# Which bank or buffer a tile gets: one tag for a whole ring, or one tag for each buffer

## The chip, the cores and the metric

The kernel runs on 1 core of one Trainium2 chip. The metric is device time in microseconds (us) of that core: 1204.38 us, the median of 3 runs (1204.35 to 1204.39). One more execution was profiled. It took 1205.93 us, and the span of its trace, from the first instruction to the last, is 1204.2 us.

## The reference

Two stages follow each other. The first is attention with pooled queries, for 8 batches and 8 heads, 1152 keys and head dimension 64:

```python
q_pool = q.reshape(B, H, S // 2, 2, D).mean(axis=3)          # 576 queries
scores = scale * np.matmul(q_pool, k.transpose(0, 1, 3, 2))
attn = exp(scores - max) / (sum + 1e-09)
attn_out = np.matmul(attn, v)                                # 8 x 8 x 576 x 64
```

The second takes the heads side by side as x (8 x 576 x 512). Each of 4 experts projects x to q, k and v of width 64, does causal attention and projects back to 512. A gate picks 2 of the 4 experts for each row and weighs them:

```python
logits = x @ w_gate; topk = the 2 largest; w = softmax over those 2
for e in range(4):
    ye = causal_softmax(scale * (x @ wq[e]) @ (x @ wk[e]).T) @ (x @ wv[e]) @ wo[e]
    out += (e in topk) * w_e * ye
```

## The kernel before, in words

**Tiling.** Heads go in 32 pairs (4 per batch). For each pair the kernel finds row maxima of rough scores (TensorE writes 128x384 tiles, VectorE reduces them, L572), then computes the scores transposed in 9 chunks of 128 keys (L325, as products of split operands qh, ql, kh, kl), exponentiates them on ScalarE into SBUF tiles called pt (L666), multiplies pt by v on TensorE (L332) and adds the pt tiles up on GpSimd into sacc (L349), for the denominators. The queries of a pair are done in two parts of 256 and 320 (QB). The end of a part takes three steps: ScalarE copies the accumulated product out of its PSUM bank into accs (L336); a second bank, den, receives the denominators, their inverse and then the product with accs (VectorE, L345); ScalarE casts den to the high half of x (L336), and VectorE subtracts that from den to get the low half of x (L345). That subtraction is the last reader of the den bank.

**The second stage.** When a batch's four pairs are there, `f_qk` projects x to the experts' queries and keys (L316, 12 matmuls for a tile, four of x's pairs times three terms; the tiles are cast to mqh and mkh). For two experts at a time it makes query and key tiles of 256 columns, then of 320. `f_mmax` (L930) computes score tiles for the row maxima, each in a bank of its own, which VectorE reduces (L956, L960). Causal attention and the output projection follow with the same helpers as in the first stage. Work on one batch's second stage is mixed with the first stage of the next pairs.

**Buffers.** Every kind of tile has a `Ring` (L128): a tag, a shape and a number of buffers. The ring `gen` has 8 buffers of 128x512 float32, which are the 8 PSUM banks: every matmul result lives in one of them. Other rings lie in SBUF: pt (11 buffers), sacc (3), kh (8), v (6) and so on.

**The order of the work.** The kernel is written out by hand. Python generators (`Flow`) stand for the steps. A loop at the end of the kernel function keeps a clock for each engine (`clk`), adds an estimated cost for every instruction it emits (`emit`, L255), and always takes the flow that can go next by these clocks. The framework runs under `tc.manual_schedule()`, so each engine gets its instructions in the order of emission. `emit` notes in each tile's record when the tile was last used by its clocks and by which engine (`u`, `ue`); `ru` is that time plus a delay for the semaphore (0.15 to 0.2 us by the table SEM). For three kinds of VectorE instruction (`port=True`, among them the subtractions that make ql and the sum of qraw, each with two operands in SBUF) `emit` moves the start behind the GpSimd instruction that its clocks show running.

When a step is through with a tile it calls `free()`, which puts the buffer's last times on the ring's list `slots`. A new tile takes the smallest entry of that list, and the clocks go on as if it had got that buffer:

```python
t = min(self.slots)
r = Res(self.pool.tile(self.shape, self.dt, tag=self.tag, name=f"{self.tag}_{self.n}", bufs=self.bufs), self)
_, r.u, r.ue = t
```

The entry holds times only. Which of the ring's buffers the tile really gets is decided by the framework, which knows the tag and the number of buffers, and keeps a timing of its own. The instruction that first writes the tile waits, by semaphore, until the former tile of the buffer that it really got has been used for the last time.

Of the kernel before, what the change touches and what calls it, by code (L numbers as in the profile page):

```python
# [104 lines left out]
class Res:  # L105


    def __init__(self, ap, ring=None):
        self.ap, self.ring, self.w, self.u = ap, ring, 0.0, 0.0
        self.we = self.ue = ""  # L110
# [10 lines left out]
        return self.u + SEM[self.ue]  # L121

    def free(self):
        self.ring.slots.append((self.ru, self.u, self.ue))
        self.ring.live -= 1


class Ring:  # L128
    def __init__(self, pool, tag, shape, dt, bufs):
        self.pool, self.tag, self.shape, self.dt, self.bufs = pool, tag, shape, dt, bufs  # L130
        self.slots, self.live, self.n = [(0.0, 0.0, "")] * bufs, 0, 0

    def avail(self, k=1):
        return sorted(self.slots)[k - 1][0] if len(self.slots) >= k else INF
# [1 line left out]
    def new(self):  # L136
        t = min(self.slots)
        self.slots.remove(t)
        self.live += 1
        self.n += 1  # L140
        r = Res(self.pool.tile(self.shape, self.dt, tag=self.tag, name=f"{self.tag}_{self.n}", bufs=self.bufs), self)
        _, r.u, r.ue = t
        return r


# [1055 lines left out]
```

## Time and profile before

| | |
|---|---|
| median of 3 runs | 1204.38 us (1204.35 to 1204.39) |
| the profiled execution | 1205.93 us, its span 1204.2 us |
| TensorE matmul (PE) busy | 1158.4 us, 96% |
| VectorE (DVE) busy | 860.6 us, 71% |
| ScalarE (ACT) busy | 704.5 us, 58% |
| GpSimd (POOL) busy | 972.0 us, 81% |
| granted TensorE clock | 0.996 of full speed |

PEld is TensorE's loading of weights, which overlaps its matmuls. The ends of matmuls are modelled, so TensorE's 96% does not mean that it could not do more in the time. A stretch in which one engine waits is worth something only if the chain of waits that ends last goes through it.

### The profile page before, as it was taken

Reading aid. Unit: us, or ns where it says so; the run is one execution under the profiler, and the core shown is the slowest. Engines: PE = TensorE matmul, PEld = TensorE weight load, DVE = VectorE, ACT = ScalarE, POOL = GpSimd, SP = SyncE. Lnnn points to the kernel's source line nnn. Section 1 sums busy time; section 2 is a strip of 40 time slices with the busy share of each in tenths; the row PEclk is TensorE's granted clock in tenths of the full one; section 3 lists DMA queues with packets and bytes.
Section 4 is the critical chain, followed back from the end, with each engine's and each line's share of the span. In section 5 each row is a group of like instructions: output and inputs, shape, how many; then the busy total and the mean of one; then the engine's idle time right before and its main releaser. Section 6 shows DMA issues by size and latency. Waiting matters only on the chain.

```text
span 1204.2 us, 29456 instructions
## 1 busy us (share of the span) xinstructions
PE 1158.4 (96%) x11233; PEld 892.0 (74%) x11233; DVE 860.6 (71%) x2113; ACT 704.5 (58%) x2036; POOL 972.0 (81%) x844
## 2 busy tenths in 40 slices
PE   6999999999999999999999999999999999999997
PEld 5676886778876787767886777866877677877785
DVE  7988667767676767777677776776767876577265
ACT  5676545765466654665556754566646665465624
POOL 4999978797699966999669987699786996889912
PEclk9999998999999999999999999999999999999999
DMA  4232212022211212122111221112211122200001
GB/s 158 80 102 69 61 54 67 16 66 76 61 54 55 69 48 61 54 60 92 32 41 54 85 82 30 44 47 85 78 41 34 60 65 87 61 15 9 8 29 45
DMA packets 40426, 70.30 MB, mean 58 GB/s; under 512 B 4871, under 2 KB 31453, under 8 KB 40285
## 3 DMA queue, kind: packets, MB, share of 16 engines
q1 hardware_dynamic: 40284, 68.43, 18.5%
q8 instruction: 88, 1.44, 0.5%
q14 instruction: 54, 0.43, 0.1%
HBM read 58.73 MB, written 9.44 MB: 57 GB/s over the span
## 4 chain that ended last, share of the span: by engine, by line
PE 61%; POOL 27%; DVE 5%; ACT 3%; issue 3%; DMA 1%; POOLq 0%; SPq 0%; DVEq 0%; ACTq 0%
PE gen L325 24%; POOL sacc L349 23%; PE gen L316 19%; PE gen L332 17%; POOL kl L349 3%; ACT pt L666 2%; POOL pt L1018 1%; DVE gen L956 1%; DVE PM L572 1%; DVE ql L345 1%; ACT pt L999 1%; PE gen L622 0%; DVE gen L734 0%; DMA qraw<-in_qT 0%; DVE gen L345 0%
## 5 line engine op out<-in xcount | busy, mean ns | idle before, releaser
L349 POOL TENSOR_TENSOR sacc<-sacc,pt 128x640 f32<-128x640 f32 (+4 forms) x588 | 828.2, 1413 | 128.6 <-ACT sacc L341 92.4
L572 DVE TENSOR_REDUCE PM<-gen 128x1 f32<-128x384 f32 x864 | 425.6, 549 | 168.7 <-PE gen L325 140.3
L666 ACT ACTIVATE pt<-gen 128x320 f32<-128x320 f32 (+1 forms) x1152 | 381.4, 432 | 137.1 <-PE gen L325 126.9
L332 PE MATMUL gen<-pt,v 128*64 128x320 f32 (+4 forms) x2752 | 355.7, 402 | 1.7 <-POOL pt L1018 0.5
L332 PEld LDWEIGHTS gen<-pt,v 128*64 128x64 f32 (+1 forms) x2752 | 192.1, 137 | 138.9 <-issue 11.8
L325 PE MATMUL gen<-qh,kh 64*128 64x320 f32 (+1 forms) x1152 | 211.8, 316 | 2.7 <-ACT accs L336 1.1
L325 PE MATMUL gen<-qh,kl 64*128 64x320 f32 (+1 forms) x1152 | 196.3, 297 | 0.0
L325 PE MATMUL gen<-RM,ON 64*128 64x320 f32 (+1 forms) x1152 | 191.6, 292 | 0.8 <-ACT RM L336 0.8
L325 PE MATMUL gen<-ql,kh 64*128 64x320 f32 (+1 forms) x1152 | 191.3, 293 | 0.0
L325 PE MATMUL gen<-kh,qh 64*128 64x384 f32 x768 | 157.1, 368 | 7.4 <-ACT qh L336 7.1
L325 PEld LDWEIGHTS gen<-qh,kh 64*128 64x128 f32 x1152 | 132.8, 185 | 33.8 <-issue 11.3
L325 PEld LDWEIGHTS gen<-RM,ON 64*128 64x128 f32 x1152 | 130.4, 186 | 1.2 <-ACT RM L336 1.0
L325 PEld LDWEIGHTS gen<-ql,kh 64*128 64x128 f32 x1152 | 129.8, 186 | 0.0
L325 PEld LDWEIGHTS gen<-qh,kl 64*128 64x128 f32 x1152 | 127.4, 186 | 0.0
L325 PEld LDWEIGHTS gen<-kh,qh 64*128 64x128 f32 x768 | 88.2, 187 | 38.1 <-issue 16.3
L316 PE MATMUL gen<-x,WH 128*128 128x320 f32 (+1 forms) x512 | 104.9, 299 | 7.4 <-DVE x L345 7.4
L349 POOL TENSOR_TENSOR kl<-kraw,kh 128x384 fp32r<-128x384 f32 x96 | 95.5, 1013 | 9.5 <-ACT mqh L336 3.4
L956 DVE CUSTOM_DVE_ANT_0 gen<-gen,mqk 64x288 f32<-64x288 f32 (+4 forms) x160 | 74.7, 503 | 25.6 <-PE gen L325 24.4
L316 PEld LDWEIGHTS gen<-x,WH 128*128 128x128 f32 x512 | 82.2, 188 | 10.6 <-issue 9.7
L332 PE MATMUL gen<-sacc,ones 128*64 128x320 f32 (+1 forms) x384 | 66.1, 425 | 13.8 <-POOL sacc L349 13.3
L336 ACT CAST x<-gen 128x256 fp32r<-128x256 f32 x64 | 25.8, 403 | 86.9 <-DVE gen L345 86.8
L316 PE MATMUL gen<-x,WL 128*128 128x320 f32 (+1 forms) x256 | 75.6, 295 | 0.0
(116 smaller groups left out, 1573.5 us busy)
## 6 DMA issues: line engine op xcount, KB each, us to landing
kraw<-in_kT SPq DMA_DIRECT2D x96, 192.0 KB
v<-in_vP SPq DMA_DIRECT2D x96, 192.0 KB
qraw<-in_qT SPq DMA_DIRECT2D x31, 576.0 KB
out<-ob SPq DMA_DIRECT2D x28, 256.0 KB
wst<-in_wall SPq DMA_DIRECT2D x8, 193.0 KB
out<-pt SPq DMA_DIRECT2D x4, 256.0 KB
RM<-nt SPq DMA_DIRECT2D x62, 2.5 KB
out<-ob SPq DMA_DIRECT2D x6, 128.0 KB
```

The costliest lines, as they stand in the source:

```text
L316: nc.tensor.matmul(o, lhsT, rhs, start=start, stop=stop)
L325: nc.tensor.matmul(o(j), l(HEAD[j]), r(HEAD[j]), start=i == 0, stop=i == len(terms) - 1)
L332: nc.tensor.matmul(o(HEAD[j]), l(j), r(j), start=start, stop=stop)
L336: nc.scalar.copy(o, i)
L345: nc.vector.tensor_tensor(o, a, b, op=op)
L349: nc.gpsimd.tensor_tensor(o, a, b, op=op)
L572: nc.vector.tensor_reduce(pm[:, i, t:t + 1], ps[:, :384], axis=AX.X, op=ALU.max)
L666: nc.scalar.activation(pts[i][:, j, :qn], st[j][:, qn * i:qn * i + qn], AF.Exp, scale=0.0625)
L956: nc.vector.tensor_tensor_reduce(p, p, mqk[:m, 384 + m - w:384 + m], 1.0, LOW, ALU.add, ALU.max, pm[:m, j, c, i:i + 1])
L999: nc.scalar.activation(pt_[:kn, j, f:qn], st[j][:kn, o - n:o], AF.Exp, scale=0.125)
L1018: nc.gpsimd.affine_select(out=sq, in_=sq, compare_op=ALU.is_ge, fill=0.0, base=0, pattern=[[0, 2], [1, kn]], channel_multiplier=-1)
```

## The change

A ring's list of free buffers now holds the buffer's number beside its times. A new tile is asked for under the tag of its ring plus that number, with one buffer under that tag. So the framework has nothing to choose: the tile gets the buffer whose entry was smallest by the emission's clocks. This holds for every ring. The smallest entry is the same as before, since the number only stands last in it, and so no clock changes, nor does the order in which instructions are emitted.

```diff
     def free(self):
-        self.ring.slots.append((self.ru, self.u, self.ue))
+        self.ring.slots.append((self.ru, self.u, self.ue, self.slot))
         self.ring.live -= 1
...
-        self.slots, self.live, self.n = [(0.0, 0.0, "")] * bufs, 0, 0
+        self.slots, self.live, self.n = [(0.0, 0.0, "", i) for i in range(bufs)], 0, 0
...
-        r = Res(self.pool.tile(self.shape, self.dt, tag=self.tag, name=f"{self.tag}_{self.n}", bufs=self.bufs), self)
-        _, r.u, r.ue = t
+
+        r = Res(self.pool.tile(self.shape, self.dt, tag=f"{self.tag}{t[3]}", name=f"{self.tag}_{self.n}", bufs=1), self)
+        _, r.u, r.ue, r.slot = t
         return r
```

## Rows read from the trace of the kernel before

**Rows 1.** The page: span, busy time by engine, chain that ended last by engine

```profile
span 1204.2 us, 29456 instructions
...
PE 1158.4 (96%) x11233; PEld 892.0 (74%) x11233; DVE 860.6 (71%) x2113; ACT 704.5 (58%) x2036; POOL 972.0 (81%) x844
...
PE 61%; POOL 27%; DVE 5%; ACT 3%; issue 3%; DMA 1%; POOLq 0%; SPq 0%; DVEq 0%; ACTq 0%
```

**Rows 2.** The waits: engine, line, released by: us in total, times, longest

```profile
PEld gen L325 <- issue: 33.0, 93, 0.5
...
PEld gen L325 <- DVE PM L572: 11.8, 49, 0.5
...
ACT pt L666 <- POOL sacc L349: 7.9, 9, 1.4
...
PE gen L316 <- DVE x L345: 7.4, 6, 1.2
PEld gen L325 <- ACT accs L336: 7.3, 15, 0.5
...
PEld gen L316 <- ACT pt L666: 5.5, 20, 0.5
...
PEld gen L622 <- ACT pt L666: 5.1, 20, 0.4
```

**Rows 3.** TensorE's timeline, 720 to 757 us: start us, us, instructions [idle before]

```profile
741.49 0.41 PE L316 MATMUL gen<-x,WH 128*128 128x256 f32 x2
...
749.36 0.76 PE L325 MATMUL gen<-mkh,mqh 64*128 64x512 f32 x6
751.36 0.47 PE L316 MATMUL gen<-x,WH 128*128 128x256 f32 x2 [1.24 <-DVE x L345]
...
752.87 0.45 PE L316 MATMUL gen<-x,WH 128*128 128x320 f32 x2
...
754.64 0.47 PE L316 MATMUL gen<-x,WH 128*128 128x320 f32 x2
...
756.41 0.27 PE L622 MATMUL gen<-ident,nm 128*10 128x128 f32 x1
```

**Rows 4.** VectorE's timeline, 747 to 757 us

```profile
748.72 0.43 DVE L345 TENSOR_TENSOR gen<-accs,gen 128x256 f32<-128x256 f32 x1
749.06 1.82 DVE L345 TENSOR_TENSOR ql<-qraw,qh 128x576 fp32r<-128x576 f32 x1
750.80 0.41 DVE L345 TENSOR_TENSOR x<-gen,x 128x256 fp32r<-128x256 f32 x1
751.14 0.68 DVE L956 CUSTOM_DVE_ANT_0 gen<-gen,mqk 128x512 f32<-128x512 f32 x1
...
754.08 0.17 DVE L618 TENSOR_REDUCE nm<-MPM 128x10 f32<-128x20 f32 x1
```

**Rows 5.** ScalarE's timeline, 747 to 757 us

```profile
749.24 0.37 ACT L336 CAST x<-gen 128x256 fp32r<-128x256 f32 x1 [1.95 <-DVE gen L345]
749.51 0.43 ACT L336 COPY accs<-gen 128x320 f32<-128x320 f32 x1
```

**Rows 6.** GpSimd's timeline, 749.2 us, and 744 to 900 us

```profile
748.71 1.55 POOL L349 TENSOR_TENSOR sacc<-sacc,pt 128x640 f32<-128x640 f32 x1
...
762.58 0.23 POOL L871 TENSOR_TENSOR gate<-v,gate 128x20 f32<-128x20 f32 x1 [5.36 <-DVE gate L871]
...
768.32 1.27 POOL L349 TENSOR_TENSOR sacc<-sacc,pt 128x512 f32<-128x512 f32 x1 [1.20 <-ACT sacc L341]
```

**Rows 7.** The chain that ended last, 744 to 770 us, and at the start

```profile
8.02 6.64 DVE PM L572 x15
...
749.15 1.73 DVE ql L345
750.88 0.34 DVE x L345
...
751.36 5.21 PE gen L316 x36
```

**Rows 8.** Groups of instructions, shapes apart: busy us, mean ns, idle before

```profile
L345 DVE TENSOR_TENSOR ql<-qraw,qh 128x576 fp32r<-128x576 f32 x31 | 39.7, 1279 | 5.6 <-PE gen L325 2.6 <-ACT qh L336 2.5
```

## The prediction, on record before the changed kernel ran

> **What bounds the kernel now.** I read the page first, then the waits, then the timeline of each engine around one wait, then the chain. The page shows matmuls busy for 1158.4 of 1204.2 us, GpSimd as the next engine with 972.0, and a chain that is 61% TensorE and 27% GpSimd [rows 1]. So time is to be had only where TensorE stands still, or where a stretch of GpSimd on the chain starts late. TensorE is idle for 1204.2 - 1158.4 = 45.8 us in all, lead-in and end included.
>
> The change concerns waits of one kind only: a tile's first writer waits until the former tile in its bank or buffer has been read. In the waits these are the rows in which TensorE waits for a reader of `gen` [rows 2]. For the weight loads they sum to 11.8 + 7.3 + 5.5 + 5.1 = 29.7 us in 49 + 15 + 20 + 20 = 104 waits, 0.29 us each. For the matmuls one row stands out: 7.4 us in 6 waits for "DVE x L345", 1.2 us each. Six waits of one length are one place that comes back in each batch's round.
>
> That place needs the timelines. The reader is to see this at 751.36: six matmuls of a row-max step begin at 749.36, and TensorE then idles 1.24 us, from 750.12 to 751.36, until VectorE has made the low half of x (750.80, 0.41 us) [rows 3, 4]. By its names this is a wait for data, but the data had been there. The matmul at 751.36 projects 256 columns of x, and a projection of the same columns ran at 741.49 [rows 3]: by `f_qk` the tiles of an expert pair come as queries 256, keys 256, queries 320, keys 320, and all of a batch's x must be there for the 320 columns. The x made at 750.80 is for the next batch. What that instruction also does is to read the den bank for the last time. So the projection got den's bank, and waited for it.
>
> Was another bank free? There are 8. Six hold the row-max tiles, which VectorE starts to read only at 751.14, behind the subtraction [rows 4]. The seventh is den. The eighth held a product that ScalarE copied into accs from 749.51 to 749.94 [rows 5], before TensorE had even ended its six matmuls. So a free bank stood unused for 751.36 - 749.94 = 1.42 us.
>
> **The change part by part.** *Instructions.* None is added, removed or moved. The number stands last in the list's entry, so the smallest entry has the same times, and the emission's clocks and its order stay as they are. SP's and GpSimd's queues keep their order too. What can change is which semaphore a first writer waits for, and when it is reached.
>
> *The six places: -7.4 us.* Which bank do the clocks take at 751.36? Both free ones are on the list, so it is the one with the earlier `ru`. I follow the emission's rules from the end of den's product (748.72 + 0.43 = 749.15 [rows 4]). ScalarE's cast of x and the copy into accs follow back to back, so accs is done within 0.8 us (749.94 [rows 5]). VectorE first makes ql, marked `port=True`. Measured, it took 1.82 us against a mean of 1.279 us [rows 4, 8], and it ended 0.62 us after the GpSimd addition of 748.71, whose 1.55 us ran to 750.26 [rows 6]. `emit` copies this: it puts such an instruction behind the GpSimd instruction that it holds to be running. Then comes the subtraction. So den's entry should be about 1.2 us later than that of the copied bank, and the clocks take the copied bank. The projection can then start when TensorE gets to it, at 750.12. Gain: the whole gap, 1.24 us, six times, 7.4 us.
>
> *Is something else late next?* The next tile, 12 matmuls on (752.87 - 751.36 = 1.51 us), would start at 751.63 and take den's bank, read by 751.21. The third would start at 754.64 - 1.24 = 753.40 and takes a row-max bank that VectorE starts to read at 751.14 and holds 0.68 us. The transposition at 756.41 would come at 755.17, and its operand nm is there at 754.08 + 0.17 = 754.25 [rows 3, 4]. So nothing takes the wait's place in the next 5 us. Is it on the path that sets the end? The chain runs through ql, the subtraction and then 36 projections of 5.21 us [rows 7]. GpSimd, the other engine on the chain, is idle behind this place: 5.36 us ended by the gate at 762.58 and 1.20 us ended by ScalarE's first sacc at 768.32 [rows 6], both fed by TensorE. It starts its next long stretch earlier with TensorE. I count the gain in full.
>
> *All other bank picks: 0, between -29.7 and +29.7 us.* The 104 waits of weight loads [rows 2] could go altogether, or as many could come. Both rules hand out the buffer that was free first, one by the framework's timing and one by the emission's. They differ only where two engines free banks within some tenths of a us. Weight loads run ahead of matmuls, so much of these waits is not TensorE's time. I take 0, near to what the rule gives in a steady state, and for the range 15 waits of 0.29 us either way, 4.3 us.
>
> *SBUF rings: 0, between -7.9 and +7.9 us.* The row that bears on them is ScalarE waiting for a pt buffer that GpSimd reads: 7.9 us in 9 waits [rows 2]. ScalarE is busy 58% [rows 1], and GpSimd's own work is what the den matmuls wait for at such times. If this cover were gone the row would be the price. Rings that one engine frees in order (kh, kl, sacc) should get the same buffers as before.
>
> *Second waits: 0, between -33.0 and +33.0 us.* A writer whose bank was read by two engines may need a further semaphore instruction. The nearest row is weight loads idle for no traced reason, 33.0 us in 93 places, 0.35 us each [rows 2]. I see no reason for a shift in the number: the same tiles with the same readers follow each other.
>
> The sum is -7.4 us against the span of 1204.2 us. The profiled execution took 1205.93 us, 1.5 us more than the median of the runs, and the median lies 0.2 us above the span. So I take the gain from the median: 1204.4 - 7.4 = 1197.0 us.
>
> **The rivals.** *The clocks choose the same bank at the six places: 1204.4 us.* For it: without the hold behind GpSimd the emission's costs would put ql at 0.67 and the subtraction at 0.34 us, so den would be done at 749.15 + 1.01 = 750.16, only 0.2 us behind the copy. A shift of the clocks of that size would turn the order where the hold is short. Against it: GpSimd works without a pause there, so the hold is there, and it is 1.1 us in the trace.
>
> The Trainium skill, Perfetto Trace Analysis, Optimization Strategy, speaks against the change too: a gap that comes back the same on the engine that should be busy can mean that there isn't PSUM enough for the next tile. By that rule the gap would stay, whichever bank is chosen, and the time too, 1204.4 us. The trace does not agree for these six: one bank was read by 749.94. For the other bank waits it may hold.
>
> *The gain is given back at GpSimd: about 1203.5 us.* GpSimd has 27% of the chain. If its long stretches began no earlier, TensorE would only wait longer for sacc. Against it stand the 5.36 and 1.20 us of idle time that end with TensorE's work.
>
> *More banks are picked better: 1192.7 us.* The 7.4 us and 15 of the 104 waits: 1204.4 - 7.4 - 4.3.
>
> *Slower: the clocks trust VectorE too early.* Place: the row-max tiles of each pair, where VectorE frees one bank per reduction, 6.64 us / 15 = 0.44 us apart [rows 7]. ql costs 0.67 us on the clocks and 1.279 us on the chip [rows 8]. Where the hold does not cover the difference, VectorE's banks look free 0.6 us before they are, the clocks prefer them to ScalarE's, and TensorE gets its bank one reduction late. Once for each of 32 pairs that is 32 x 0.44 = 14.1 us, less 7.4: 1211.1 us. It decides from 17 such waits on (7.4 / 0.44). Against it: reductions and copies on the clocks have costs near the measured ones, and VectorE's stalls come from GpSimd, which the hold is there for.
>
> **How the numbers follow.** Forecast as worked out, 1195 to 1200 us: 0.55. More banks picked better: 0.10. Same bank at the six places or all banks in use: 0.16. Given back: 0.04. Slower: 0.15. A measurement of this kernel can tell about 0.2%, 2.4 us, from no change. Faster by more: 0.55 + 0.10 = 0.65. Within: 0.16 + 0.04 = 0.20. Slower: 0.15. The range goes from 1192.7 up to the case of no change with half a us on it, 1192.7 to 1205.0; it leaves out the slower case and a little more at the low end. The likeliest case's own range is 1195 to 1200.
>
> **What would show it.** Right: the row of TensorE waiting for "DVE x L345" is gone or below 1 us, the chain has no ql ahead of the projections any more, matmuls are as busy as before in a span 7 us shorter, and GpSimd's idle time ahead of the gate is no longer than before. Wrong in the first step: the row still stands with 6 waits. Wrong in the second: the row is gone, but weight loads' waits for row-max readers grow above 11.8 us by as much, or TensorE's waits for sacc do. A time above 1205 with the row gone would mean new waits elsewhere.

## The result, and the profile after

The changed kernel takes 1193.16 us (median of 4 runs, 1191.78 to 1195.37), the kernel before on the same chip 1204.39 us (4 runs, 1204.35 to 1204.52). The ratio is 0.9909, with a 95% interval of 0.9893 to 0.9924: 11.2 us faster, where 7.4 were forecast. The time lies within the range, below the likeliest case's own range of 1195 to 1200.

Both kernels issue the same instructions in the same order on every engine. There are 21 semaphore instructions fewer (29456 to 29435). What differs is which buffer a tile gets: counted in the two programs, 787 of the 2472 `gen` tiles and 97 of the 693 `pt` tiles follow another tile in their buffer than before, and no tile of any other ring.

The page of the changed kernel, to be held against [rows 1]:

```profile
span 1191.3 us, 29435 instructions
...
PE 1153.4 (97%) x11233; PEld 891.0 (75%) x11233; DVE 855.8 (72%) x2113; ACT 704.0 (59%) x2036; POOL 974.6 (82%) x844
...
PE 64%; POOL 25%; ACT 4%; DVE 3%; issue 3%; DMA 0%; POOLq 0%; SPq 0%; ACTq 0%; DVEq 0%
```

The span is 12.9 us shorter. TensorE is idle for 1191.3 - 1153.4 = 37.9 us, 7.9 less than before, and its matmuls count as busy 5.0 us less. That second number matters below: not all of the gain was in a gap that one could see.

The waits of the changed kernel (engine, line, released by: us in total, times, longest; its lines are one further down than in [rows 2]):

```profile
PEld gen L326 <- issue: 31.5, 89, 0.5
...
PE gen L333 <- POOL sacc L350: 13.4, 16, 1.6
...
PEld gen L326 <- DVE PM L573: 7.6, 32, 0.5
...
PEld gen L326 <- ACT pt L667: 4.5, 12, 1.7
...
PEld gen L623 <- ACT pt L667: 3.1, 14, 0.2
ACT pt L667 <- POOL sacc L350: 3.0, 4, 1.4
PEld gen L317 <- DVE PM L573: 2.9, 11, 0.3
...
PEld gen L326 <- DVE MPM L961: 2.6, 6, 0.5
PEld gen L623 <- DVE PM L573: 2.5, 8, 0.4
...
PEld gen L326 <- ACT accs L337: 2.5, 5, 0.5
...
PEld gen L317 <- ACT pt L667: 2.1, 10, 0.4
...
PEld gen L317 <- ACT accs L337: 1.5, 6, 0.4
```

The row "PE gen L316 <- DVE x L345" with its six waits of 1.2 us is gone. The four rows of weight loads that summed to 29.7 us in 104 waits [rows 2] now sum to 7.6 + 2.5 + 2.1 + 3.1 = 15.3 us in 61. But they are four of twelve, and the waits went to other rows. In the kernel before three of these were small:

```profile
PEld gen L325 <- ACT pt L666: 1.1, 4, 0.4
...
PEld gen L622 <- DVE PM L572: 0.4, 2, 0.2
...
PEld gen L316 <- DVE PM L572: 0.3, 1, 0.3
```

They are now 4.5, 2.5 and 2.9 us, and L326 <- MPM L961 and L317 <- accs are new. Over all rows in which a weight load for scores, projections or transpositions (L325, L316, L622 before) waits for a reader of a bank (ScalarE's pt and accs, VectorE's PM and MPM) the sum is 38.1 us in 125 waits before and 36.5 us in 124 after. So these waits were passed round, hardly lessened. ScalarE's wait for a `pt` buffer that GpSimd reads fell from 7.9 to 3.0 us.

The place of [rows 3 to 6] in the changed kernel comes 8.67 us earlier (751.36 - 742.69). TensorE's timeline (start us, us, instructions, idle before), its weight load, and then the timelines of VectorE, ScalarE and GpSimd:

```profile
742.00 0.77 PE L326 MATMUL gen<-mkh,mqh 64*128 64x512 f32 x6
742.69 0.50 PE L317 MATMUL gen<-x,WH 128*128 128x256 f32 x2
...
744.22 0.46 PE L317 MATMUL gen<-x,WH 128*128 128x320 f32 x2
```

```profile
742.69 0.30 PEld L317 LDWEIGHTS gen<-x,WH 128*128 128x128 f32 x2 [0.22 <-ACT accs L337]
```

```profile
741.71 1.81 DVE L346 TENSOR_TENSOR ql<-qraw,qh 128x576 fp32r<-128x576 f32 x1
743.44 0.41 DVE L346 TENSOR_TENSOR x<-gen,x 128x256 fp32r<-128x256 f32 x1
```

```profile
742.16 0.43 ACT L337 COPY accs<-gen 128x320 f32<-128x320 f32 x1
```

```profile
753.93 0.23 POOL L872 TENSOR_TENSOR gate<-v,gate 128x20 f32<-128x20 f32 x1 [3.50 <-DVE gate L872]
...
759.66 1.27 POOL L350 TENSOR_TENSOR sacc<-sacc,pt 128x512 f32<-128x512 f32 x1 [1.17 <-ACT sacc L342]
```

The reader is to see three things. The projection starts at 742.69, straight behind the six matmuls and 0.10 us behind the end of ScalarE's copy (742.16 + 0.43 = 742.59), and its weight load waited 0.22 us for that copy: it has the copied product's bank. The new row of six waits for accs at L317 is this place in six batches. VectorE still ends the low half of x late, at 743.85, and nobody waits for it. GpSimd's idle time ahead of the gate is 3.50 us where it was 5.36 [rows 6], so the time was passed on.

The chain of the changed kernel around it (start us, us, what), against [rows 7]:

```profile
737.72 4.35 PE gen L333 x32
742.07 0.70 PE gen L326 x6
742.76 5.15 PE gen L317 x36
747.92 0.11 PE gen L623
```

No ql and no x stand in it any more.

### The profile page after: what moved, and what is told of

The parts are those of the page before. It is cut to its first block, busy times and chain, and to the rows that moved or that the text cites. A ratio compares the mean times of both kernels' runs of the same rounds, so it can differ in the third digit from the quotient of the medians.

```text
span 1191.3 us, 29435 instructions
## 1 busy us (share of the span) xinstructions
PE 1153.4 (97%) x11233; PEld 891.0 (75%) x11233; DVE 855.8 (72%) x2113; ACT 704.0 (59%) x2036; POOL 974.6 (82%) x844
## 4 chain that ended last, share of the span: by engine, by line
PE 64%; POOL 25%; ACT 4%; DVE 3%; issue 3%; DMA 0%; POOLq 0%; SPq 0%; ACTq 0%; DVEq 0%
PE gen L326 25%; POOL sacc L350 22%; PE gen L333 20%; PE gen L317 19%; ACT pt L667 2%; POOL kl L350 2%; DVE PM L573 2%; POOL pt L1019 1%; ACT pt L1000 1%; PE gen L623 1%; ACT sacc L342 0%; DMA qraw<-in_qT 0%; POOL gate L872 0%; DVE gen L735 0%; DVE gen L346 0%
## 5 line engine op out<-in xcount | busy, mean ns | idle before, releaser
L326 PE MATMUL gen<-qh,kh 64*128 64x320 f32 (+1 forms) x1152 | 215.7, 315 | 2.6 <-ACT pt L667 1.4
L326 PE MATMUL gen<-qh,kl 64*128 64x320 f32 (+1 forms) x1152 | 200.3, 297 | 0.0
L326 PE MATMUL gen<-RM,ON 64*128 64x320 f32 (+1 forms) x1152 | 194.2, 292 | 0.8 <-ACT RM L337 0.8
L326 PE MATMUL gen<-ql,kh 64*128 64x320 f32 (+1 forms) x1152 | 193.9, 292 | 0.0
L326 PE MATMUL gen<-kh,qh 64*128 64x384 f32 x768 | 158.7, 368 | 7.7 <-ACT qh L337 6.9
L326 PEld LDWEIGHTS gen<-qh,kh 64*128 64x128 f32 x1152 | 136.3, 185 | 32.1 <-issue 11.2
L326 PEld LDWEIGHTS gen<-RM,ON 64*128 64x128 f32 x1152 | 133.0, 186 | 1.2 <-ACT RM L337 1.1
L326 PEld LDWEIGHTS gen<-ql,kh 64*128 64x128 f32 x1152 | 132.4, 185 | 0.0
L326 PEld LDWEIGHTS gen<-qh,kl 64*128 64x128 f32 x1152 | 129.3, 185 | 0.0
L326 PEld LDWEIGHTS gen<-kh,qh 64*128 64x128 f32 x768 | 89.6, 187 | 38.6 <-issue 14.9
L317 PE MATMUL gen<-x,WH 128*128 128x320 f32 (+1 forms) x512 | 104.6, 299 | 0.2 <-ACT accs L337 0.2
L317 PEld LDWEIGHTS gen<-x,WH 128*128 128x128 f32 x512 | 81.9, 188 | 3.0 <-ACT accs L337 1.5
L317 PE MATMUL gen<-x,WL 128*128 128x320 f32 (+1 forms) x256 | 75.4, 294 | 0.0
```

Source lines behind the costliest of these rows:

```text
L317: nc.tensor.matmul(o, lhsT, rhs, start=start, stop=stop)
L326: nc.tensor.matmul(o(j), l(HEAD[j]), r(HEAD[j]), start=i == 0, stop=i == len(terms) - 1)
```

## The experiments

Theory A says that the gain is a matter of which PSUM bank a tile gets, the six places above all. The rivals: a tag of one's own changes something as such (fewer semaphores, another way of releasing); the gain comes from SBUF rings; the emission's clocks are wrong about VectorE, so that another choice would be better still. All times below stand against 1204.6 to 1204.7 us for the kernel before on the same chip; the experiments ran on three chips, e1 to e5, e6 to e9 and e10 with e11, and the kernel before ran beside each group.

**Parts of the change.** e1 gives only `gen` tags of its own, e2 every ring but `gen` (`!=` in the first line):

```diff
+        own = self.tag == "gen"
+        tag, bufs = (f"{self.tag}{t[3]}", 1) if own else (self.tag, self.bufs)
-        r = Res(self.pool.tile(..., tag=f"{self.tag}{t[3]}", ..., bufs=1), self)
+        r = Res(self.pool.tile(..., tag=tag, ..., bufs=bufs), self)
```

> Only the ring gen (the PSUM banks) has a tag for each buffer; every SBUF ring has one tag, as before. Theory A (the gain is the choice of banks): as the changed kernel, 1193.2 us within 2 us. Rival B (the 97 of 693 pt tiles that get another SBUF buffer bring part of it, for ScalarE waits less for GpSimd): up to 5 us of the 11.2 us are lost, 1196 to 1198 us. Rival C (one-buffer tags by themselves give fewer semaphore waits): between the two kernels, since most rings are back at one tag, though gen has most of the tiles.

> The other half: every SBUF ring has a tag for each buffer, gen has one tag of 8 banks as before. Theory A: 1204.4 us within 1 us, no gain, and the six waits of TensorE for the low half of x are back at 7.4 us. Rival B: 1199 to 1202 us. Rival C: some us faster than before.

e4 writes out the banks that `gen` had in the kernel before as a list, and exchanges them at the six places only. The other rings keep the change:

```diff
+        i = int(BANKS[self.n - 1]) if self.tag == "gen" else t[3]
+        self.ids.remove(i)
-        r = Res(self.pool.tile(..., tag=f"{self.tag}{t[3]}", ..., bufs=1), self)
+        r = Res(self.pool.tile(..., tag=f"{self.tag}{i}", ..., bufs=1), self)
```

> Every tile of gen gets by a written list the bank that it had in the kernel before, but at the six places the projection's tile takes the bank of the copied product and the next tile takes den's (12 of 2472 tiles get another predecessor than before). Theory A: the six gaps of 1.24 us are gone and all else is as before: 1204.4 - 7.4 = 1197.0 us. A rival by which the gain at these places is given back later (at GpSimd): 1201 to 1204 us. If the six were the whole change: 1193 us.

e5 is the changed kernel with the six places put back to den's bank:

```diff
+SIX = (659, 968, 1276, 1585, 1893, 2202)
...
+        if self.tag == "gen" and self.n + 1 in SIX:
+            o = min(self.slots)
+            self.slots.remove(o)
+            self.slots.append((*o[:3], t[3]))
+            t = (*t[:3], o[3])
```

> The changed kernel, but at the six places the projection's tile gets den's bank and the next tile the copied product's (12 of 2472 tiles get another predecessor than in the changed kernel). Theory A: the six gaps come back, 1193.2 + 7.5 = 1200.7 us. If the gaps were hidden by other work in the changed kernel's timing: 1193 to 1195 us. If the six were the whole change: 1204 us.

| kernel | median us (range) | ratio, 95% interval |
|---|---|---|
| e1, `gen` alone | 1193.67 (1193.57 to 1196.08) | 0.9916, 0.9903 to 0.993 |
| e2, all but `gen` | 1201.48 (1200.91 to 1205.84) | 0.998, 0.9971 to 0.9989 |
| e4, six places and the other rings | 1194.69 (1193.48 to 1196.25) | 0.992, 0.9907 to 0.9934 |
| e5, all but the six places | 1200.18 (1198.77 to 1203.05) | 0.9966, 0.9953 to 0.9978 |

e1 and e5 came out where theory A had put them. e2 did not: no gain was expected, within 1 us of 1204.4, and 1201.48 us lies in rival B's range, so the SBUF rings bring something too. e4 was put at 1197.0 us, which left out that it keeps the change of the other rings; it lies 6.8 us below e2.

The six places are worth 1200.18 - 1193.16 = 7.0 us by e5 and 1201.48 - 1194.69 = 6.8 us by e4. Their row in the waits of e2 and of e5, then the projection's first matmul in TensorE's timeline of e5 and, without a wait, of e4:

```profile
PE gen L319 <- DVE x L348: 7.4, 6, 1.2
```

```profile
PE gen L325 <- DVE x L354: 7.4, 6, 1.2
```

```profile
746.13 0.36 PE L325 MATMUL gen<-x,WH 128*128 128x256 f32 x1 [1.23 <-DVE x L354]
```

```profile
744.61 0.39 PE L351 MATMUL gen<-x,WH 128*128 128x256 f32 x1
```

To split the rest I took the stretch between the same two matmuls in each trace, one behind the start-up and one ahead of the end (the bounds lie within 0.12 us of them). All of it ran at a granted clock of 1.00 (the column behind the five busy times). Stretch, length, busy time of TensorE, its weight loads, VectorE, ScalarE and GpSimd; the kernel before first, then the changed one, e5, e2, e4, e1 and a second trace of the changed kernel (e9, below):

```profile
303.90:1150.00 846.10, 824.99 (x8140) 638.10 (x8139) 595.54 (x1463) 502.29 (x1458) 708.03 (x615) 1.00 0.18 54
```

```profile
302.10:1137.70 835.60, 821.96 (x8140) 638.16 (x8139) 592.52 (x1463) 502.08 (x1458) 710.63 (x616) 1.00 0.18 55
```

```profile
300.40:1143.50 843.10, 822.26 (x8141) 638.38 (x8139) 594.65 (x1463) 502.04 (x1458) 706.83 (x616) 1.00 0.18 55
```

```profile
301.90:1146.50 844.60, 823.46 (x8140) 637.09 (x8139) 594.07 (x1463) 502.09 (x1458) 708.21 (x615) 1.00 0.18 55
```

```profile
303.30:1140.40 837.10, 823.26 (x8140) 637.22 (x8139) 592.28 (x1463) 502.19 (x1458) 711.77 (x616) 1.00 0.18 55
```

```profile
301.50:1138.30 836.80, 823.50 (x8140) 638.94 (x8139) 593.01 (x1463) 502.48 (x1458) 710.40 (x615) 1.00 0.18 55
```

```profile
302.10:1138.20 836.10, 822.12 (x8140) 638.28 (x8139) 592.93 (x1463) 502.25 (x1458) 711.47 (x616) 1.00 0.18 55
```

The change shortens this stretch by 846.1 - 835.6 = 10.5 us. The six places give 843.1 - 835.6 = 7.5, and 844.6 - 837.1 = 7.5 where nothing else of `gen` is changed. The other banks of `gen` give 837.1 - 835.6 = 1.5, the other rings 846.1 - 844.6 = 1.5. These are steps of one way from the kernel before to the changed one (e2, e4), so they must add up; what checks them is the other way, 7.5 by e5 and 836.8 - 835.6 = 1.2 for the other rings by e1. The two traces of the changed kernel differ by 836.1 - 835.6 = 0.5 us, and each term of 1.2 to 1.5 us is known to about that much, as far as two traces tell.

No tile of any ring but `gen` and `pt` follows another one than before, so the last term is taken to be `pt`. ScalarE's wait for a `pt` buffer goes the same way: 7.9 us before and 8.3 in e1, 3.0 in the changed kernel and 2.3 in e2 (e1 first, then e2):

```profile
ACT pt L669 <- POOL sacc L352: 8.3, 8, 1.5
```

```profile
ACT pt L669 <- POOL sacc L352: 2.3, 3, 1.5
```

What the ten semaphore instructions fewer of e2 do to this term was not told apart.

The columns show a second thing. TensorE's idle time, length less busy time, is 21.1 us before, 21.1 in e2 and 20.8 in e5, and 13.6, 13.8 and 13.3 in the changed kernel, e4 and e1: the six places took it all. The smaller gains stand in the busy column (825.0 before, 823.5 in e2, 823.3 in e4, 822.0 in the changed kernel). The same matmuls at the same clock count as busy for 3.0 us less: what a better bank or buffer saved there was never shown as idle time of its matmuls. The ends of matmuls are modelled, so these columns don't tell how it was spent.

**The tag or the order.** e6 keeps the tags but takes the `gen` bank that has been on the list longest, by the order of the calls of `free()` in the emission:

```diff
+        i = self.ids[0] if self.tag == "gen" else t[3]
```

> Own tags, but a gen tile gets the bank that stands longest on the list in the order in which the emission calls free(), whatever the clocks say; at the six places that is den's bank again, as in the kernel before. Theory A (the clocks' order of time is what helps): the six gaps are back, 7.4 us, and other picks lose some more, 1200 to 1205 us. Rival D (any order fixed at emission does, as long as the framework doesn't choose): 1193 us.

It took 1207.69 us (1206.14 to 1209.91), ratio 1.0025 (1.0014 to 1.0036), slower than before and above the 1200 to 1205 us that theory A had given; rival D is out. The six waits are back, and those for VectorE's reductions stand at 12.6 us (11.8 before):

```profile
PEld gen L331 <- DVE PM L578: 12.6, 55, 0.5
...
PE gen L322 <- DVE x L351: 7.4, 6, 1.2
```

With own tags and the wrong order the gain is gone, so the tags don't make it. That they do nothing at all is not shown by e6, whose order loses time too. e4 against e2 bounds it: tags of their own for `gen` together with the six exchanges took 7.5 us off the long stretch, and the six waits alone are 7.4 us. Own tags with exactly the banks of the kernel before were not run.

**How good the clocks are.** e7 takes the bank whose last reader ended first in the trace of the changed kernel, written out as a list as in e4. 564 tiles follow another tile in their bank than in the changed kernel.

> Own tags, and for gen a written list: each tile gets the bank whose last reader ended first in the trace of the changed kernel (564 of 2472 tiles get another predecessor than in the changed kernel). Theory A with clocks that are nearly right: 0 to 3 us below the changed kernel, 1190 to 1193 us. If the clocks' picks were still often wrong: 5 us below or more. If the picks shift the times so much that a list taken from one trace is out of date: no gain, 1193 to 1196 us.

It took 1193.83 us (1192.63 to 1195.43), ratio 0.9911 (0.9897 to 0.9925). The changed kernel ran once more beside it:

> The changed kernel as it is, beside the others on the same chip: 1193.2 us, within 2 us.

That took 1193.58 us (1192.19 to 1193.86), ratio 0.9905 (0.9891 to 0.9919). The measured order brings nothing that could be told from it. Its weight loads waited less for banks (31.1 us in 112 waits over the rows summed above, against 36.5 in 124), and the time is the same. So theory A's forecast of up to 3 us less did not come. 1193.83 us lies in the range of the last case, a list out of date; whether that, or clocks that leave nothing to gain, is the reason stays open.

e8 lets the choice, and nothing else, count VectorE's banks as free 0.6 us early, e10 0.6 us late, e11 0.2 us early:

```diff
+        o = min(self.slots + [t], key=lambda s: (s[0] - (0.6 if s[2] == "DVE" else 0.0), s))
+        if self.tag == "gen" and o is not t:
+            self.slots.remove(o)
+            self.slots.append((*o[:3], t[3]))
+            t = (*t[:3], o[3])
```

> The changed kernel, but for the choice of a gen bank alone a bank freed by VectorE counts as free 0.6 us earlier than the clocks say (1452 tiles get another predecessor; not at the six places, where the entries lie 1.56 us apart). This is the prediction's slower rival made on purpose: clocks that trust VectorE too early. By its price of 0.44 us for a pick gone wrong, and one or two of them in each of 32 pairs, 14 to 28 us above the changed kernel: 1207 to 1221 us. If banks are free long enough before they are needed: 1193 to 1197 us.

> As the kernel in which VectorE's banks counted as free 0.6 us early, but 0.6 us late (1300 tiles get another predecessor than in the changed kernel, none of them at the six places). Theory A (what counts is the true order in time, and the clocks are near it): slower in this direction too, 5 to 14 us above the changed kernel, 1198 to 1207 us. Rival E (the clocks still trust VectorE too early by some tenths): less than half of the loss in the other direction, 1190 to 1199 us.

> VectorE's banks count as free 0.2 us early for the choice (544 tiles get another predecessor). Theory A: order within 0.2 us hardly matters, 1193 to 1197 us. If each wrong pick costs the same whatever the shift (13.7 us for 1452 tiles): 13.7 x 544 / 1452 = 5 us, 1199 us.

| kernel | banks that differ | median us (range) | ratio, 95% interval |
|---|---|---|---|
| e8, 0.6 us early | 1452 | 1207.32 (1205.62 to 1209.22) | 1.002, 1.0011 to 1.0029 |
| e10, 0.6 us late | 1300 | 1201.2 (1200.64 to 1205.77) | 0.9979, 0.997 to 0.9988 |
| e11, 0.2 us early | 544 | 1193.73 (1193.33 to 1195.96) | 0.9912, 0.9898 to 0.9926 |

Their waits, e8, e10 and e11 in this order:

```profile
PEld gen L331 <- DVE PM L578: 32.7, 139, 1.0
...
PEld gen L331 <- DVE MPM L962: 10.6, 14, 1.2
...
PE gen L331 <- DVE MPM L962: 6.6, 11, 0.9
```

```profile
PEld gen L331 <- ACT pt L672: 28.2, 61, 1.7
...
PE gen L331 <- ACT pt L672: 11.8, 41, 1.4
```

```profile
PEld gen L331 <- DVE PM L578: 15.2, 64, 0.6
```

Too early, and TensorE waits for VectorE's banks (32.7 us where it was 7.6). Too late, and it waits for ScalarE's (28.2 us where it was 4.5, and 11.8 us of matmuls; this trace is of the slowest of e10's twelve runs, 1205.77 us). Over the rows summed above it is 63.8 us in 217 waits for e8, 57.4 in 155 for e10 and 41.2 in 142 for e11, against 36.5 in 124. All three times lie in the first of the ranges given for them. Both ways lose, 13.7 and 7.6 us against the second run of the changed kernel (the kernel before took 1204.68 us beside e8 and beside e10), so among these shifts the clocks' own order is the best, with e11 as good; less than 0.6 us late was not tried. e11 is the lesson on size: its row for VectorE is twice that of the changed kernel (15.2 against 7.6 us), and its time is the same. A weight load that waits 0.24 us ahead of its matmul is mostly not TensorE's time.

No experiment gave a version that beats the changed kernel.

## Why the prediction was right in its mechanism and short in its sum

**The six places: right, in mechanism and size.** -7.4 us were predicted. The stretch shows 7.5 by both ways of taking them alone, the medians 6.8 and 7.0. The reading that carried it was that a wait named after data ("DVE x") was a wait for a bank, since the same instruction reads den's bank for the last time. e5 shows it: against the changed kernel only the bank differs, and the wait is back. That the clocks put the copied bank first is in the emission's list too: 305.02 against 306.58 at the first place, 733.65 against 735.22 at the fourth, 1.6 us apart where I had put 1.2.

**Nothing late behind it: right.** The 320-column tiles follow at the old distance, 744.22 - 742.69 = 1.53 us against 1.51, without a wait. GpSimd's idle time ahead of the gate did not grow, so the rival "given back at GpSimd" fell.

**Where it failed: "All other bank picks: 0" and "SBUF rings: 0".** These two terms were mis-sized; the first measures -1.5 us in the stretch, the second -1.2 to -1.5. Behind the first stood the sentence that the two rules "differ only where two engines free banks within some tenths of a us". 787 picks differ; in 386 of them the bank of the kernel before stood on the list as well, and in 309 of these the two entries lie within 0.3 us, as the sentence says (in the others that bank had already been given out). It does not hold at the six places themselves, 1.6 us apart. The step that failed is the price: it was taken from four of twelve rows of weight-load waits. Over all such rows the waits stayed as they were (125 and 124), and yet 1.5 us went, out of time in which matmuls count as busy. Behind the second stood the cover by GpSimd. The price named for it was the row of 7.9 us; 4.9 of them went, and 1.2 to 1.5 came out in time. By the medians all but the six places give 1204.57 - 1200.18 = 4.4 us (e5); with the 7.0 us of the six by e5 that makes 11.4, the whole within the scatter of the runs. About 1.4 us of the 4.4 lie ahead of the stretch and behind it, where the clock varies (last section), and could not be split.

I had looked for gains only in TensorE's idle time. The six places were all that showed there; the other 3 us of the stretch were inside matmuls counted as busy.

**Second waits: right at 0 or a little below.** 21 semaphore instructions went, and the row of weight loads that waited for "issue" fell from 33.0 us in 93 to 31.5 in 89. The row of the projections' weight loads that waited for "issue" fell from 14.9 us in 21 to 5.8 in 14; it stands at 14.8 in e2 and 12.9 in e5, so most of that is the six gaps once more, seen on the weight loads.

**The rivals.** "The same bank at the six places" and with it "too little PSUM" fell: the gap went with the same 8 banks. The Trainium skill, Perfetto Trace Analysis, Optimization Strategy, takes consistent bubbles for a possible sign of too little PSUM. The trace does not agree here: 7.5 us of them came from taking a bank that was still being read while another had been read out. "More banks are picked better", at 1192.7 us, is what the time looks like, 0.5 us off; I had given it 0.10. That is luck in part: its mechanism, 15 waits fewer, did not come (125 and 124), and some of the gain is `pt`, not banks. "Slower, the clocks trust VectorE too early" names a mechanism that exists: e8 makes it happen, with 139 waits in the row that has 32 in the changed kernel, and costs 13.7 us; 107 waits more in that row (93 over all rows summed above) cost what I had priced at 32 of 0.44 us. The changed kernel's clocks don't trip it.

**What stays open.** Why the framework's timing put den's bank first at the six places was not tried; e6 takes it there too, by the order of the calls of `free()`. The 1.5 us of the other banks could not be tied to single waits.

## What to carry to other kernels

Where an emission keeps clocks of its own, let them name the buffer too; two ledgers that order the same buffers differently cost 0.9% here, with not one instruction changed but semaphores. Read a wait on TensorE twice: the instruction that ends it may be the data's maker or the bank's last reader, and only the timelines of all engines tell whether another bank was free. Then size such a change by the matmuls' waits and by the same stretch in both traces: single rows of weight-load waits mislead, since the waits move to other rows and are mostly not TensorE's time, and idle time alone misses what is hidden in busy time.

## What the runs showed of the hardware that was not expected

The changed kernel's four runs scatter by 3.6 us (1191.78 to 1195.37, the faster the higher the mean granted clock, 0.999 to 0.995). The kernel before stood within 0.2 us beside them, but in the 15 runs beside e1 to e5 it went from 1203.46 to 1206.12 us, so it is not shown that the change makes them scatter. Part of it can be seen in one place, 190 to 210 us, where TensorE idles 0.7 and 0.5 us between row-max and projections. The same stretch in the kernel before, the changed one and e5 (the granted clock is the column behind the five busy times):

```profile
190.00:210.00 20.00, 18.58 (x166) 12.76 (x162) 14.16 (x47) 8.93 (x27) 16.51 (x13) 0.83 0.30 90
```

```profile
190.00:210.00 20.00, 18.25 (x166) 12.19 (x164) 15.11 (x51) 10.02 (x32) 16.54 (x13) 0.91 0.29 90
```

```profile
190.00:210.00 20.00, 18.11 (x181) 12.44 (x179) 16.05 (x52) 11.10 (x36) 16.64 (x13) 1.00 0.30 90
```

A mean of 0.83 or 0.91 is part of the stretch at the lower of the two levels, 1.2 GHz. The changed kernel and e5 are the same program up to their first exchanged bank, near 310 us, and yet stood at 0.91 and 1.00 here, behind the same idle time. From the same matmul behind that idle time (196.03 and 195.59) to the start of the long stretch, the one took 302.10 - 196.03 = 106.07 us and the other 300.40 - 195.59 = 104.81. At 107 to 120 us the two stood at 0.87 and 1.00, behind an idle time of 1.4 us in both. So 1.3 us of a run hang on the clock that the place at 190 to 210 us happens to get, about a tenth of what the change is worth, and differences of that size need several runs or a stretch at full clock.
